# Low parts on VectorE instead of GpSimd, and a layer border without decoding, in a fused retention and two-layer MLP kernel

## The chip, the core and the metric

The kernel runs on one core of a Trainium2 chip. The metric is the device time of one execution in microseconds (us). Three runs of the kernel before gave 601.18, 601.47 and 603.46, a median of 601.47. One more execution was taken with the hardware profiler and is the source of every row below.

The engines are named as in the profile: PE is TensorE (matmuls), PEld its weight loads, DVE is VectorE, ACT is ScalarE, POOL is GpSimd, SP is the engine that issues the transfers here. SBUF is the on-chip memory; PSUM holds what PE writes.

## The reference

A retention (linear attention with a decay for each head), and then two MLP layers over its 1536 tokens of 512 values:

```
for t in range(S):                       # B=2, H=8, S=768, D=64
    state = gamma * state + k[t] (x) v[t]
    y[t] = scale * q[t] @ state
x = y as 1536 x 512
h = x @ w_in;  x = (max(h,0) + alpha*min(h,0)) @ w_out          # layer 1, d_ff = 2048
h = x @ w_in;  P = a0 + a1 h + a2 h^2 + a3 h^3                  # layer 2, d_ff = 2048
Q = 1 + |b0||h| + |b1| h^2;  out = (P / (Q + 1e-6)) @ w_out
```

The eight-byte weights are read as pairs of 32-bit words.

## The kernel before

**Retention.** 12 chunks of 128 tokens, six for each batch element. A chunk has a stage "b" (`att_b`: scores `sc` on PE, DVE multiplies them by the decay mask into `s` at L131, ACT scales q for the state at L136, and POOL multiplies q by `dq_sb` at L137) and a stage "c" (`att_c`: state products `st`, output `y` on PE at L160 and L170, DVE adds `st` to the state `R` at L177 or L179, ACT copies `y` to the high part `xh` at L183, DVE writes the low part `xl` at L184). `att_k` scales k on POOL (L118). Chunks 0 to 4 stand in a prologue; a table `stages` puts the others between the steps of layer 1.

**Splitting.** A matmul operand is a high part (a rounded copy) and a low part (what the copy left over), and each product is three matmuls: high by high, high by low, low by high. So whatever feeds PE (x, the weights, the activations g) is copied by ACT and then subtracted by DVE or POOL.

**Decoding.** 64 weight halves of 128x512 (two layers, 16 ff tiles m, n=0 for w_in and n=1 for w_out) come in as word pairs `r` by SP (L240). Decoding one takes ACT L248 (the absolute value), three DVE operations on the words (L254, L258, L262), ACT L273 (the high part `wh`) and one subtraction at L280 (the low part `wl`). L279 chooses its engine: POOL for every n=1, for the first four ff tiles, and for the halves that start late; else DVE. The table `START` says in which half step a decoding begins; its word operations come one half step later, the copy two, the low part three.

**Steps.** 96 steps, each an ff tile m for a block of 512 tokens: `pe_h` (12 matmuls, L305), the activation, `pe_out` (12 matmuls into four PSUM accumulators, L322). `SWEEPS` orders them: in layer 1 the first `GA` ff tiles (list A) for blocks 0 and 1 with partial sums spilled, then all 16 for block 2, then the rest (list B) for blocks 1 and 0, added to the spilled sums. Layer 2 does likewise with `GC` = 10, blocks 2, 1 and then 0. `pe_h` runs two steps ahead of `pe_out`. In layer 1 the activation is ACT L340 and L341, DVE L346, ACT L351, DVE L356. In layer 2 it is ACT L367 to L369, DVE L373, ACT L380 and L381, DVE L382, L383, L391, L392, L395, ACT L402 (high part of g) and POOL L404 (its low part). `evac` ends a sweep; where it adds (L419) in layer 1 it also makes the two parts of the next layer's x at once, the high part on ACT (L431) and the low one on POOL (L433).

Everything is emitted in one hand-written order (`manual_schedule`), and each engine works through its own queue in that order. Half step 2i stands before `pe_out(i)` and 2i+1 behind it. Tiles share 42 slots of SBUF, and the oldest free one is used next.

Of the kernel before, what the change touches and what calls it, by code (L numbers as in the profile page):

```python
# [7 lines left out]
F32 = mybir.dt.float32  # L8
# [3 lines left out]
ALU = mybir.AluOpType  # L12
# [6 lines left out]
NK = 4  # L19
NCH = 12  # L20
# [3 lines left out]
QC = 1.0 + 1e-6  # L24
NWARM = 8
NSLOT = 42
GA = 6
GC = 10


# [1 line left out]
def tile_fused(  # L32
# [18 lines left out]
    nc = tc.nc  # L51
# [9 lines left out]
    def alloc(nm, dt=F32):  # L61
        k = free.pop(0)
        t = one.tile([P, 1024], dt, tag=f"s{k}", name=nm)
        slot[id(t)] = (k, t)
        return t

    def drop(t):
        free.append(slot.pop(id(t))[0])
# [13 lines left out]
    dq_sb = one.tile([P, 512], F32, tag="dq", name="dq_sb")  # L82
# [5 lines left out]
    def xs(hl, b, ks, sl):  # L88
        return (xh, xl)[hl][b][:, ks, sl]
# [30 lines left out]
    def att_b(c, bank):  # L120
        a = att[c]
        ps = [bank(f"sc{c}_{e}") for e in range(2)]
        for j in range(NK):
            js = slice(j * P, (j + 1) * P)
            for e in range(2):
                es = slice(64 * e, 64 * e + 64)
                nc.tensor.matmul(ps[e][:, js], a["t"][es, js], a["q"][es, js], start=True, stop=True)  # L127
        a["s"] = alloc(f"s{c}")
        for e in range(2):
            es = slice(512 * e, 512 * e + 512)  # L130
            nc.vector.tensor_tensor(out=a["s"][:, es], in0=ps[e], in1=dm_sb[:, es], op=ALU.mult)  # L131
        if c % CPB > 0:
            for j in range(NK):
                js = slice(j * P, (j + 1) * P)
                o = 8 * CPB + 4 * (c % CPB) + j
                nc.scalar.mul(a["q"][:, js], a["q"][:, js], cst_sb[:, o:o + 1])  # L136
            nc.gpsimd.tensor_tensor(out=a["q"], in0=a["q"], in1=dq_sb, op=ALU.mult)  # L137

    def att_c(c, ybank, pbank):
        a = att.pop(c)  # L140
# [51 lines left out]
    Z = {}  # L192
# [5 lines left out]

    A, B = range(0, GA), range(GA, NF)
    C, D = range(0, GC), range(GC, NF)  # L200
# [9 lines left out]
    first, final = {}, {}  # L210
# [5 lines left out]
    START = {}  # L216
    for m in A:
        START[0, m, 0], START[0, m, 1] = 2 * m - 9, 2 * m - 4
    for j, m in enumerate(B):
        START[0, m, 0], START[0, m, 1] = 8 + 4 * j, 10 + 4 * j  # L220
    for m in range(NF):
        for n in range(2):
            k = 2 * m + n
            if k < 8:
                t = 52 + 3 * k
            elif k < 20:
                t = 76 + (5 * (k - 8)) // 3
            else:
                t = 98 + (11 * (k - 20)) // 2
            START[1, m, n] = t  # L230
    SEQ = sorted(START, key=lambda e: (START[e], e))
    loaded = [0, 0]

    def load_next(depth):
        while loaded[0] < len(SEQ) and loaded[0] - loaded[1] < depth:
            k = loaded[0]
            loaded[0] += 1
            l, m, n = SEQ[k]
            r = alloc(f"r{k}", U32)
            nc.sync.dma_start(out=r, in_=SRC[l][n][m].bitcast(U32))  # L240
            words = r.rearrange("p (f t) -> p f t", t=2)
            raw[k] = (words[:, :, 0], words[:, :, 1], r)
# [7 lines left out]
    def w_word(k, part):  # L250
        lo, hi, r = raw[k]
        zu = Z[k].bitcast(U32)
        if part == 0:
            nc.vector.tensor_scalar(  # L254
                out=zu, in0=zu, scalar1=3, scalar2=None, op0=ALU.logical_shift_left
            )
        elif part == 1:
            nc.vector.scalar_tensor_tensor(  # L258
                out=zu, in0=lo, scalar=29, in1=zu, op0=ALU.logical_shift_right, op1=ALU.bitwise_or
            )  # L260
        else:
            nc.vector.scalar_tensor_tensor(  # L262
                out=zu, in0=hi, scalar=0x80000000, in1=zu, op0=ALU.bitwise_and, op1=ALU.bitwise_or
            )
            drop(r)
            loaded[1] += 1
# [9 lines left out]
    def w_lo(k):  # L276
        l, m, n = SEQ[k]
        hi, lo = W[l, m, n]
        eng = nc.gpsimd if n or (l == 0 and m < 4) or START[SEQ[k]] >= 2 * N1 else nc.vector  # L279
        eng.tensor_tensor(out=lo, in0=Z[k], in1=hi.bitcast(F32), op=ALU.subtract)  # L280
        if k % 2 == 1:
            drop(ZP[k // 2])

# [7 lines left out]
    acc = {}  # L291
# [3 lines left out]
    ALL = slice(0, TB)  # L295
# [111 lines left out]
    def evac(i):  # L407
        l, b, m, _, how = STEPS[i]
        if how == "add" or (how == "final" and l == 0):
            part_b = part.pop((l, b), None)  # L410
        else:
            part_b = [alloc(f"p{i}_{n}") for n in range(2)]
        if how == "spill":
            part[l, b] = part_b
        if part_b:
            ps = [part_b[k // 2][:, 512 * (k % 2):512 * (k % 2) + 512] for k in range(NK)]
        for k in range(NK):
            if how == "add":
                nc.vector.tensor_tensor(out=ps[k], in0=acc[0][k], in1=ps[k], op=ALU.add)  # L419
            elif how == "spill" or l == 1:  # L420
                if k % 2 == 0:
                    nc.scalar.copy(ps[k], acc[0][k])
                else:
                    nc.vector.tensor_copy(ps[k], acc[0][k])
            if how != "spill" and l == 1:
                t0 = b * TB + k * P
                nc.sync.dma_start(out=out[t0:t0 + P, :], in_=ps[k])
            if how != "spill" and l == 0:
                src = ps[k] if how == "add" else acc[0][k]
                hap = xs(0, b, k, ALL)  # L430
                nc.scalar.copy(hap, src)  # L431
                eng = nc.gpsimd if how == "add" else nc.vector
                eng.tensor_tensor(out=xs(1, b, k, ALL), in0=src, in1=hap.bitcast(F32), op=ALU.subtract)  # L433
        if how != "spill" and part_b:
            for t in part_b:
                drop(t)


    def rbank(nm):
        return ring.tile([P, 512], F32, tag="ring", name=nm)  # L440
# [4 lines left out]
    N1 = NB * NF  # L445
# [7 lines left out]
    def half(t, scalar_last=None, between=None):  # L453
        evs = dec.get(t, ())

        def each(nm):
            return [e[1] for e in evs if e[0] == nm]

        for e in each("abs"):
            w_abs(e)  # L460
        for e in each("hi"):
            w_hi(e)
        if scalar_last:
            scalar_last()
        for e in each("word"):
            w_word(e, 0)
        for e in each("lo"):
            w_lo(e)
        for e in each("word"):
            w_word(e, 1)  # L470
        if between:
            between()
        for e in each("word"):
            w_word(e, 2)
        load_next(4 if t < 2 * N1 else 2)

    with tc.manual_schedule():
# [3 lines left out]
        ps = rbank("warm")  # L481
# [42 lines left out]


        stages = {-4: ("c", 4)}
        for c in range(5, NCH):
            t = 3 * (c - 5) - 3 + (c > 7)
            stages[t] = ("b", c)
            stages[t + 2] = ("c", c)  # L530

        def stage(t):
            if t not in stages:
# [119 lines left out]
```

## Time and profile before

| what | value |
|---|---|
| median of 3 runs | 601.47 us (601.18 to 603.46) |
| the profiled execution, its span | 605.27 us, 603.5 us |
| PE busy | 581.3 us (96%), 2944 matmuls |
| DVE busy | 484.7 us (80%), 688 operations |
| ACT busy | 360.4 us (60%) |
| POOL busy | 157.9 us (26%), 121 operations |
| mean granted PE clock | 0.988 |

Busy shares are means over stages with different limits, and PE's own are modelled ends of pipelined matmuls; the tables by stretch below count matmuls, which is a better measure of what PE got done. A table by stretch gives the busy us of each engine and the number of its operations, then the granted clock, the share of the DMA engines and GB/s. A chain of waits gives the start, the us on the chain, and what stood there. A timeline gives start, duration, engine, line and operation, then idle time before it and what ended it in brackets.

### The profile page before, as it was taken

To read this page: it belongs to the slowest core of one execution; us is meant where nothing else is said; L and a number is where in the kernel's file an instruction comes from. 1 tells how busy PE (TensorE), PEld (TensorE's weight loads), DVE (VectorE), ACT (ScalarE), POOL (GpSimd) and SP (SyncE) were. 2 spreads that over 40 slices of the span, in tenths; PEclk is the share of its full clock that TensorE was granted. 3 is DMA by queue.
4 is the path that set the end of the run, shared out by engine and by line. 5 is a ranking of instruction groups with operands and counts; after the bars stand their busy time and mean duration, and the time that the engine had idled before them with its cause. 6 is when DMAs were issued, how large, how long until landed. Compare 5 with 4: busy or idle time off the path is not lost.

```text
span 603.5 us, 7942 instructions
## 1 busy us (share of the span) xinstructions
PE 581.3 (96%) x2944; PEld 475.5 (79%) x2944; DVE 484.7 (80%) x688; ACT 360.4 (60%) x637; POOL 157.9 (26%) x121
## 2 busy tenths in 40 slices
PE   7797899999999999999999799999999999999997
PEld 7676778888888888888888578878887888888885
DVE  3979877887777446455887999999999999987786
ACT  3545445555544445445565677777778777776673
POOL 2543331210101000004021443233323332322220
PEclk8999899999999999999999989999999999999999
DMA  8995433223341211211342001011102100010011
GB/s 302 363 401 210 141 104 106 71 70 106 105 141 36 70 36 35 71 49 60 136 140 104 1 36 35 2 36 35 35 1 71 35 1 1 1 70 2 31 40 71
DMA packets 18760, 50.64 MB, mean 84 GB/s; under 512 B 2592, under 2 KB 2592, under 8 KB 18720
## 3 DMA queue, kind: packets, MB, share of 16 engines
q1 hardware_dynamic: 18720, 50.13, 23.8%
q8 instruction: 23, 0.38, 0.2%
q14 instruction: 17, 0.14, 0.1%
HBM read 46.97 MB, written 3.15 MB: 83 GB/s over the span
## 4 chain that ended last, share of the span: by engine, by line
PE 64%; DVE 21%; ACT 7%; issue 5%; DMA 1%; POOL 1%; SPq 0%; DVEq 0%; ACTq 0%; POOLq 0%
PE h L305 30%; PE acc L322 30%; DVE as L392 3%; DVE z L258 3%; DVE as L373 3%; DVE as L391 2%; ACT rr L380 2%; ACT rr L381 2%; DVE z L262 2%; DVE z L254 1%; PE y L160 1%; PE sc L127 1%; PE y L170 1%; DVE as L395 1%; DMA kv<-in_kn_dram 1%
## 5 line engine op out<-in xcount | busy, mean ns | idle before, releaser
L305 PE MATMUL h<-xl,wh 128*128 128x512 f32 x384 | 150.7, 393 | 1.8 <-DVE xl L184 1.8
L305 PE MATMUL h<-xh,wh 128*128 128x512 f32 x384 | 151.6, 395 | 0.0
L305 PE MATMUL h<-xh,wl 128*128 128x512 f32 x384 | 150.5, 392 | 0.0
L322 PE MATMUL acc<-wh,g 128*128 128x512 f32 x384 | 128.1, 395 | 5.4 <-ACT g L402 4.4
L322 PE MATMUL acc<-g,wh 128*128 128x512 f32 x384 | 118.9, 391 | 0.0
L280 POOL TENSOR_TENSOR wl<-z,wh 128x512 fp32r<-128x512 f32 x42 | 60.0, 1430 | 188.9 <-ACT wh L273 178.9
L404 POOL TENSOR_TENSOR g<-as,g 128x512 fp32r<-128x512 f32 x46 | 60.9, 1323 | 155.4 <-ACT g L402 123.9
L322 PEld LDWEIGHTS acc<-wh,g 128*128 128x128 f32 x384 | 71.9, 189 | 24.4 <-ACT g L402 5.3
L305 PEld LDWEIGHTS h<-xl,wh 128*128 128x128 f32 x384 | 72.8, 190 | 17.0 <-DVE xl L184 2.1
L305 PEld LDWEIGHTS h<-xh,wl 128*128 128x128 f32 x384 | 72.8, 190 | 15.4
L305 PEld LDWEIGHTS h<-xh,wh 128*128 128x128 f32 x384 | 72.8, 189 | 15.5 <-issue 0.2
L322 PEld LDWEIGHTS acc<-g,wh 128*128 128x128 f32 x384 | 71.7, 188 | 15.1 <-ACT z L248 0.2
L273 ACT CAST wh<-z 128x512 fp32r<-128x512 f32 x64 | 39.6, 618 | 71.7 <-DVE z L262 71.7
L322 PE MATMUL acc<-wl,g 128*128 128x512 f32 x192 | 75.2, 392 | 0.0
L322 PE MATMUL acc<-g,wl 128*128 128x512 f32 x192 | 74.9, 390 | 0.2 <-POOL wl L280 0.2
L346 DVE SCALAR_TENSOR_TENSOR np<-np,nalpha_sb 128x512 f32<-128x512 f32 x48 | 36.7, 764 | 38.0 <-ACT np L341 38.0
L356 DVE TENSOR_TENSOR g<-np,g 128x512 fp32r<-128x512 f32 x48 | 42.2, 879 | 24.6 <-ACT g L351 22.8
L258 DVE SCALAR_TENSOR_TENSOR z<-r,z 128x512 uint32<-128x512 uint32 x64 | 55.0, 859 | 1.7
L340 ACT ACTIVATE np<-h 128x512 f32<-128x512 f32 x48 | 28.6, 595 | 46.1 <-PE h L305 46.1
L262 DVE SCALAR_TENSOR_TENSOR z<-r,z 128x512 uint32<-128x512 uint32 x64 | 47.6, 744 | 1.7
L373 DVE SCALAR_TENSOR_TENSOR as<-as,bb_sb,rr 128x512 f32<-128x512 f32 x48 | 42.0, 876 | 8.4 <-ACT rr L368 8.4
L392 DVE SCALAR_TENSOR_TENSOR as<-as,ab_sb,rr 128x512 f32<-128x512 f32 x48 | 48.4, 1008 | 0.0
(53 smaller groups left out, 775.0 us busy)
## 6 DMA issues: line engine op xcount, KB each, us to landing
r<-in_w1i_dram SPq DMA_DIRECT2D x16, 512.0 KB, 4.1
r<-in_w1o_dram SPq DMA_DIRECT2D x16, 512.0 KB, 4.2
r<-in_w2i_dram SPq DMA_DIRECT2D x16, 512.0 KB, 3.3
r<-in_w2o_dram SPq DMA_DIRECT2D x16, 512.0 KB, 3.2
qk<-in_qT_dram SPq DMA_DIRECT2D x12, 256.0 KB, 5.6
qk<-in_kT_dram SPq DMA_DIRECT2D x12, 256.0 KB, 6.0
kv<-in_kn_dram SPq DMA_DIRECT2D x12, 256.0 KB, 5.8
kv<-in_vn_dram SPq DMA_DIRECT2D x12, 256.0 KB, 6.2
```

The lines of the kernel that those rows point to most:

```text
L258: nc.vector.scalar_tensor_tensor(out=zu, in0=lo, scalar=29, in1=zu, op0=ALU.logical_shift_right, op1=ALU.bitwise_or)
L262: nc.vector.scalar_tensor_tensor(out=zu, in0=hi, scalar=0x80000000, in1=zu, op0=ALU.bitwise_and, op1=ALU.bitwise_or)
L273: nc.scalar.copy(hi, Z[k])
L280: eng.tensor_tensor(out=lo, in0=Z[k], in1=hi.bitcast(F32), op=ALU.subtract)
L305: nc.tensor.matmul(ps, w[:, ks], xs(hl, b, k, ALL), start=(n == 0), stop=(n == 11))
L322: nc.tensor.matmul(acc[0][k], a, c, start=(begin and n == 0), stop=(end != "" and n == 2))
L340: nc.scalar.activation(n, h, AF.Relu, scale=-1.0)
L346: nc.vector.scalar_tensor_tensor(out=p, in0=n, scalar=nalpha_sb[:, m:m + 1], in1=p, op0=ALU.mult, op1=ALU.add)
L356: nc.vector.tensor_tensor(out=gl, in0=p, in1=gh.bitcast(F32), op=ALU.subtract)
L373: nc.vector.scalar_tensor_tensor(out=s, in0=s, scalar=bb_sb[:, 1:2], in1=r, op0=ALU.mult, op1=ALU.add)
L392: nc.vector.scalar_tensor_tensor(out=a, in0=a, scalar=ab_sb[:, 0:1], in1=r, op0=ALU.add, op1=ALU.mult)
L404: eng.tensor_tensor(out=gl, in0=a, in1=gh.bitcast(F32), op=ALU.subtract)
```

## The change

1. The low parts of the weights and the product of q with `dq_sb` are always made by DVE. POOL keeps L118 and the low part of g in layer 2.
2. Where a layer 1 sweep ends by adding, the two parts of the next x are no longer made there. Their four pieces go on a list, `later`; each even half step takes one, ACT copying and DVE subtracting.
3. `GA` is 5 instead of 6, and list B has eleven ff tiles, whose decodings start every 3.4 half steps instead of every 4, from half step 6.
4. Layer 2's first 20 weight halves start at 52, 56, ... 72 and then at every half step from 76 to 89 (before: to 94); the other 12 start from 100, every 5.25 half steps (before: from 98, every 5.5).
5. The stages of chunks 5 to 11 have a table of their own, up to three half steps earlier.

Lines move by one to ten: L305 becomes L304, L322 L321, L280 L279, L346 L345, L356 L355, L373 L372, L404 L403, L419 L418, and the split of x is at L440 and L441.

```diff
-GA = 6
+GA = 5
...
-            nc.gpsimd.tensor_tensor(out=a["q"], in0=a["q"], in1=dq_sb, op=ALU.mult)
+            nc.vector.tensor_tensor(out=a["q"], in0=a["q"], in1=dq_sb, op=ALU.mult)
...
-        START[0, m, 0], START[0, m, 1] = 8 + 4 * j, 10 + 4 * j
+        START[0, m, 0], START[0, m, 1] = 6 + (17 * j) // 5, 8 + (17 * j) // 5
...
-            elif k < 20:
-                t = 76 + (5 * (k - 8)) // 3
+            elif k < 20:
+                t = 76 + k - 6
             else:
-                t = 98 + (11 * (k - 20)) // 2
+                t = 100 + (21 * (k - 20)) // 4
...
-        eng = nc.gpsimd if n or (l == 0 and m < 4) or START[SEQ[k]] >= 2 * N1 else nc.vector
-        eng.tensor_tensor(out=lo, in0=Z[k], in1=hi.bitcast(F32), op=ALU.subtract)
+        nc.vector.tensor_tensor(out=lo, in0=Z[k], in1=hi.bitcast(F32), op=ALU.subtract)
...
+            if how == "final" and l == 0:
+                split_x(b, k, acc[0][k])
+        if how == "add" and l == 0:
+            for k in range(NK):
+                later.append((b, k, ps[k], part_b[k // 2] if k % 2 else None))
...
+    def split_x(b, k, src, t=None):
+        hap = xs(0, b, k, ALL)
+        nc.scalar.copy(hap, src)
+        nc.vector.tensor_tensor(out=xs(1, b, k, ALL), in0=src, in1=hap.bitcast(F32), op=ALU.subtract)
...
+        if later and t % 2 == 0:
+            split_x(*later.pop(0))
...
-            t = 3 * (c - 5) - 3 + (c > 7)
+        for c, t, u in ((5, -3, -2), (6, -1, 1), (7, 2, 4), (8, 5, 7), (9, 8, 10), (10, 11, 13), (11, 14, 15)):
```

DVE's queue at the start, before: from the low part `xl` of chunk 5 to the scores of chunk 6. `r`, `z`: weight words; `np`, `g`: activation of a step; `s`: masked scores; `wl`: low part of a weight.

```order
L184 TENSOR_TENSOR xl_79<-y_469,xh_76 128x4x128
L254 TENSOR_SCALAR z_431<-z_431 128x512
L258 SCALAR_TENSOR_TENSOR z_431<-r_309,z_431 128x512
L262 SCALAR_TENSOR_TENSOR z_431<-r_309,z_431 128x512
L346 SCALAR_TENSOR_TENSOR np_495<-np_495,nalpha_sb 128x512
L254 TENSOR_SCALAR z_490<-z_490 128x512
L258 SCALAR_TENSOR_TENSOR z_490<-r_379,z_490 128x512
L356 TENSOR_TENSOR g_521<-np_495,g_521 128x512
L262 SCALAR_TENSOR_TENSOR z_490<-r_379,z_490 128x512
L131 TENSOR_TENSOR s_540<-sc_0_530,dm_sb 128x512
L131 TENSOR_TENSOR s_540<-sc_1_531,dm_sb 128x512
```

The same place now, from the `xl` of chunk 5:

```order
L184 TENSOR_TENSOR xl_79<-y_470,xh_76 128x4x128
L131 TENSOR_TENSOR s_501<-sc_0_491,dm_sb 128x512
L131 TENSOR_TENSOR s_501<-sc_1_492,dm_sb 128x512
L254 TENSOR_SCALAR z_431<-z_431 128x512
L279 TENSOR_TENSOR wl_0_275<-z_337,wh_0_274 128x512
L258 SCALAR_TENSOR_TENSOR z_431<-r_309,z_431 128x512
L262 SCALAR_TENSOR_TENSOR z_431<-r_309,z_431 128x512
L345 SCALAR_TENSOR_TENSOR np_509<-np_509,nalpha_sb 128x512
L254 TENSOR_SCALAR z_504<-z_504 128x512
L279 TENSOR_TENSOR wl_3_507<-z_431,wh_3_506 128x512
L258 SCALAR_TENSOR_TENSOR z_504<-r_379,z_504 128x512
```

The scores of chunk 6 follow the low part of chunk 5 at once now. From there to the low part of chunk 6 the queue holds 22 rows before (its last ones are `R` and `xl`) and 15 now: fewer decodings stand in between, and in exchange low parts `wl` do.

PE's queue at chunk 11, before and now: the last output of the retention and what comes next. `acc`: the accumulators of `pe_out`; `h`: those of `pe_h`, which here reads the block that chunk 11 completes.

```order
L160 MATMUL y_1186<-s_1136,kv_990 64x128 x8
L170 MATMUL y_1186<-qk_989,R 128x128 x4
L322 MATMUL acc_0_995<-g_1123,wh_3_492 128x512 x2
L322 MATMUL acc_0_995<-g_1123,wl_3_493 128x512
L322 MATMUL acc_1_996<-g_1123,wh_3_492 128x512 x2
```

```order
L160 MATMUL y_1115<-s_1095,kv_944 64x128 x8
L170 MATMUL y_1115<-qk_943,R 128x128 x4
L304 MATMUL h_1140<-xh_77,wh_0_274 128x512
L304 MATMUL h_1140<-xl_80,wh_0_274 128x512
L304 MATMUL h_1140<-xh_77,wl_0_275 128x512
```

The 12 matmuls of a `pe_out` that followed are gone from this place: the `pe_h` that needs chunk 11's `xh` and `xl` is next.

DVE's queue at the layer border, before: from the adds of the last layer 1 sweep to the end of step 49's activation.

```order
L419 TENSOR_TENSOR p_1_928<-acc_3_2385,p_1_928 128x512
L382 TENSOR_TENSOR as_2785<-as_2785,h_2763 128x512
L383 SCALAR_TENSOR_TENSOR as_2785<-as_2785,ab_sb,h_2763 128x512
L254 TENSOR_SCALAR z_2724<-z_2724 128x512
L280 TENSOR_TENSOR wl_9_2782<-z_2724,wh_9_2781 128x512
L258 SCALAR_TENSOR_TENSOR z_2724<-r_2647,z_2724 128x512
L262 SCALAR_TENSOR_TENSOR z_2724<-r_2647,z_2724 128x512
L391 SCALAR_TENSOR_TENSOR as_2785<-as_2785,rr 128x512
L392 SCALAR_TENSOR_TENSOR as_2785<-as_2785,ab_sb,rr 128x512
L395 SCALAR_TENSOR_TENSOR as_2785<-as_2785 128x512
```

And now:

```order
L418 TENSOR_TENSOR p_1_877<-acc_3_2325,p_1_877 128x512
L381 TENSOR_TENSOR as_2793<-as_2793,h_2776 128x512
L382 SCALAR_TENSOR_TENSOR as_2793<-as_2793,ab_sb,h_2776 128x512
L390 SCALAR_TENSOR_TENSOR as_2793<-as_2793,rr 128x512
L391 SCALAR_TENSOR_TENSOR as_2793<-as_2793,ab_sb,rr 128x512
L394 SCALAR_TENSOR_TENSOR as_2793<-as_2793 128x512
L441 TENSOR_TENSOR xl_78<-p_0_876,xh_75 128x512
```

Four decoding operations no longer stand inside this activation, and the first piece of the deferred split stands behind it.

## Rows read from the trace of the kernel before

**Rows 1.** Table by stretch: length; PE, PEld, DVE, ACT, POOL; clock, DMA share, GB/s.

```profile
36.60:71.60 35.00, 30.07 (x203) 23.65 (x204) 33.64 (x42) 18.68 (x37) 14.74 (x11) 0.95 0.69 250
330.00:360.00 30.00, 25.54 (x107) 20.30 (x106) 29.15 (x39) 20.02 (x35) 14.48 (x11) 0.94 0.05 18
350.00:540.00 190.00, 189.47 (x829) 154.84 (x829) 182.69 (x250) 141.96 (x235) 64.97 (x47) 1.00 0.07 23
540.00:570.00 30.00, 30.00 (x134) 24.86 (x133) 23.50 (x36) 20.03 (x34) 6.51 (x5) 1.00 0.09 32
```

**Rows 2.** Chain of waits: start, us on the chain, what.

```profile
43.63 1.68 DVE z L258
...
59.11 0.34 DVE z L254
59.45 0.60 DVE wl L280
...
62.77 1.31 PE sc L127 x14
...
127.59 2.72 PE h L305 x12
```

**Rows 3.** One line's operations: count, ns min/median/max.

```profile
L258 DVE SCALAR_TENSOR_TENSOR z<-r,z x64: 679/693/1772, 18.9 to 518.9; 128x512 uint32<-128x512 uint32 x64
L392 DVE SCALAR_TENSOR_TENSOR as<-as,ab_sb,rr x48: 737/747/1847, 332.8 to 594.1; 128x512 f32<-128x512 f32 x48
L383 DVE SCALAR_TENSOR_TENSOR as<-as,ab_sb,h x48: 747/748/750, 328.8 to 592.8; 128x512 f32<-128x512 f32 x48
L280 DVE TENSOR_TENSOR wl<-z,wh x22: 681/684/1771, 59.4 to 339.3; 128x512 fp32r<-128x512 f32 x22
```

**Rows 4.** Timeline of DVE and POOL, first and last stretched operations of the start.

```profile
38.59 1.30 POOL L137 TENSOR_TENSOR qk<-qk,dq_sb 128x512 f32<-128x512 f32 x1 [6.76 <-ACT qk L136]
38.93 1.25 DVE L254 TENSOR_SCALAR z<-z 128x512 uint32<-128x512 uint32 x1
...
52.82 1.50 POOL L118 TENSOR_TENSOR kv<-kv,cst_sb 128x512 f32<-128x512 f32 x1
53.33 1.53 DVE L356 TENSOR_TENSOR g<-np,g 128x512 fp32r<-128x512 f32 x1
...
69.95 1.61 DVE L356 TENSOR_TENSOR g<-np,g 128x512 fp32r<-128x512 f32 x1
```

**Rows 5.** Groups by line: count, busy us and mean ns, idle before.

```profile
L280 POOL TENSOR_TENSOR wl<-z,wh 128x512 fp32r<-128x512 f32 x42 | 60.0, 1430 | 188.9 <-ACT wh L273 178.9 <-DMA r<-in_w2i_dram 10.0
L137 POOL TENSOR_TENSOR qk<-qk,dq_sb 128x512 f32<-128x512 f32 x10 | 13.5, 1352 | 54.7 <-ACT qk L136 30.7 <-issue 23.6 <-ACT xh L183 0.5
```

**Rows 6.** Timeline after chunk 8's output: the two parts of x.

```profile
89.06 0.59 ACT L183 CAST xh<-y 128x512 fp32r<-128x512 f32 x1 [2.64 <-PE y L170]
89.94 0.69 DVE L184 TENSOR_TENSOR xl<-y,xh 128x512 fp32r<-128x512 f32 x1
```

**Rows 7.** Timeline in layer 1, step 35's low part and its `pe_out`.

```profile
258.45 0.69 DVE L356 TENSOR_TENSOR g<-np,g 128x512 fp32r<-128x512 f32 x1
266.15 0.61 PE L322 MATMUL acc<-g,wh 128*128 128x512 f32 x2
```

**Rows 8.** Timeline at the border.

```profile
336.54 5.68 POOL L433 TENSOR_TENSOR xl<-p,xh 128x512 fp32r<-128x512 f32 x4
339.31 1.77 DVE L280 TENSOR_TENSOR wl<-z,wh 128x512 fp32r<-128x512 f32 x1
341.01 1.77 DVE L258 SCALAR_TENSOR_TENSOR z<-r,z 128x512 uint32<-128x512 uint32 x1
346.46 0.50 PE L322 MATMUL acc<-wh,g 128*128 128x512 f32 x1 [3.99 <-ACT g L402]
```

**Rows 9.** Timeline in layer 2, stretched operations.

```profile
359.68 1.78 DVE L392 SCALAR_TENSOR_TENSOR as<-as,ab_sb,rr 128x512 f32<-128x512 f32 x1
368.09 1.78 DVE L373 SCALAR_TENSOR_TENSOR as<-as,bb_sb,rr 128x512 f32<-128x512 f32 x1
```

More of the change, by code (lines that the diff above doesn't have):

```diff
@@ L223, in tile_fused @@
             k = 2 * m + n
-            if k < 8:
-                t = 52 + 3 * k
+            if k < 6:
+                t = 52 + 4 * k
             elif k < 20:
-                t = 76 + (5 * (k - 8)) // 3
+                t = 76 + k - 6
             else:
-                t = 98 + (11 * (k - 20)) // 2
+                t = 100 + (21 * (k - 20)) // 4
             START[1, m, n] = t
@@ L427, in evac @@
                 nc.sync.dma_start(out=out[t0:t0 + P, :], in_=ps[k])
[L428 to L434, printed above, removed]
+            if how == "final" and l == 0:
[3 more added lines that the diff above has]
+                later.append((b, k, ps[k], part_b[k // 2] if k % 2 else None))
+        elif how != "spill" and part_b:
             for t in part_b:
                 drop(t)
+    later = []
+    def split_x(b, k, src, t=None):
+        hap = xs(0, b, k, ALL)
+        nc.scalar.copy(hap, src)
+        nc.vector.tensor_tensor(out=xs(1, b, k, ALL), in0=src, in1=hap.bitcast(F32), op=ALU.subtract)
+        if t is not None:
+            drop(t)
     def rbank(nm):
@@ L526, in tile_fused @@
         stages = {-4: ("c", 4)}
-        for c in range(5, NCH):
-            t = 3 * (c - 5) - 3 + (c > 7)
+        for c, t, u in ((5, -3, -2), (6, -1, 1), (7, 2, 4), (8, 5, 7), (9, 8, 10), (10, 11, 13), (11, 14, 15)):
             stages[t] = ("b", c)
-            stages[t + 2] = ("c", c)
+            stages[u] = ("c", c)
         def stage(t):
```

## The prediction

> **What bounds the kernel now.** I read the table by stretch first. In an undisturbed stretch PE issues 134 matmuls in 30 us [rows 1], and twelve of them, a `pe_h` or a `pe_out`, take 2.72 us on the chain [rows 2]; so a matmul is 0.227 us and a step (24) 5.44 us. Against that rate PE falls behind in three places. At the start of layer 1 (36.6 to 71.6) it is busy 30.07 of 35.00 us at a granted clock of 0.95, while DVE is busy for 33.64. At the border (330 to 360) it issues 107 matmuls where 134 would fit: 27 x 0.227 = 6.1 us lost. In layer 2 (350 to 540) it is busy 189.47 of 190, with DVE at 182.69: a balance that DVE just loses [rows 1]. So DVE is the second limit at all three places, and I ask what makes it long.
>
> The chain of waits answers for the start: between 43 and 63 us DVE stands on it, until a PE row (62.77, scores) ends that [rows 2]. Its rows differ: the same L258 takes 1.68 at 43.63, and a low part 0.60 at 59.45. One line's operations give the reason a size: L258 and L392 have a median of 0.69 and 0.75 and a maximum of 1.77 and 1.85, while L383, which reads `h` from PSUM, never leaves 0.747 to 0.750. L280 on DVE is 0.684, with a maximum of 1.77 [rows 3]. The timeline gives the culprit: DVE's L254 at 38.93 and L356 at 53.33 are long, and beside each a POOL operation runs (L137 from 38.59, L118 from 52.82). A long operation is one that shares its time with a POOL operation [rows 4]. Between 36.6 and 71.6 ten DVE operations are long, the first and the last in [rows 4]; by what POOL ran, eight belong to L280 and L137, two to L118.
>
> The Trainium skill, page "SBUF — State Buffer", section "SBUF: two separate sides", says that GpSimd and a VectorE operation with two SBUF inputs share one pair of ports as an exclusive lock, held for a whole instruction, and that the other engine is fully blocked meanwhile. The trace agrees on who is hit (L383 is not); what it shows of the size is about one microsecond per meeting, less than POOL's 1.43 us. By that rule taking work from POOL frees more than it adds.
>
> **The change part by part.**
>
> *Low parts and L137 move to DVE.* POOL loses 42 L280 (60.0 us, 1.43 each), 10 L137 (1.35 each) [rows 5] and the eight low parts of x (the four of the second sweep take 5.68 us, [rows 8]). DVE gets these 60, at 0.68 [rows 3], or 0.60 from one to the next where they queue [rows 2]. That is +36 us of DVE in all, against about 50 us by which I find 56 long operations too long over the kernel, nearly 40 of it by the moved POOL lines. What counts is where.
>
> *Start, first sweep.* Removed: eight meetings of 0.92 each (L356 at 69.95 takes 1.61, undisturbed 0.69) = -7.4. Added up to 71.6: two L137 and four more low parts, 6 x 0.60 = +3.6. Moved: list A's sixth tile leaves this stretch and list B comes in at other places, which makes one decoding less up to the last scores: 0.34 [rows 2] + 2 x 0.69 [rows 3] and the small gaps between, -1.75. The order agrees: 15 rows from chunk 5's low part to chunk 6's, 22 before. Sum -5.5. PE bounds it: what can be won there is its idle 4.9 us plus 5% clock of 35 (1.75) = 6.7. Just outside this stretch I add -0.5 before and -0.4 behind it, where PE also waits for word operations or a low part. Transfers: list B's words are asked for two half steps earlier and 15% denser. DMA has ended 10.0 of 188.9 us of POOL's idle time before a low part, all of it in layer 2 [rows 5], and the share here is 0.69 [rows 1]; I cost it at nothing, with +1 as bound.
>
> *A new wait at chunk 11.* `pe_h` of the block that chunk 11 completes follows its output directly. It needs `xh` and `xl`: after a `y`, 0.59 on ACT and then 0.69 on DVE, with hand-offs 1.6 us in all (89.06 to 90.63) [rows 6]. High-by-high matmuls need only `xh`, but the second one needs `xl`. I take +1.4; bounds 0.6 (`xl` hidden) and 2.5 (DVE late by one or two queued operations). Behind the wait in PE's queue stands all of the next step. **Start in all: -6.4 + 1.4 = -5.0**, bounds -7 and -1.
>
> *Layer 1, middle.* Two sweeps of spare time: step 35's `g` is ready at 259.14 and its `pe_out` starts at 266.15, 7 us later [rows 7]. Low parts (0.60 each, 2 per 6.8 half steps) use none of PE's time here: cost 0. For half steps 76 to 89 the new table starts a decoding in every half step: two per step, each 0.34 + 3 x 0.60 by queue cadence, and the activation 0.66 + 0.60 make 5.5 to 5.7 us of DVE against 5.44. Seven steps of +0.2 eat 1.4 of 7 us, with the early dip perhaps 5: cost 0. By full durations (0.34 + 3 x 0.69 twice, 0.75 + 0.69) it would be 6.3 us, 6 us too much over seven steps, and with the spare time partly used already a stall of up to 4.5: that is a bound, and a rival.
>
> *Border.* Before, step 49's activation has four decoding operations inside it, two of them long (L280 and L258, 1.77 each) since POOL is making low parts of x for 5.68 us at that time; PE waits 3.99 us for `g` [rows 8]. All of it goes: 0.34 + 1.77 + 1.77 + 0.69 is 4.6 us on this one chain, more than the wait. Also, POOL's low part of step 49's `g` is no longer queued behind four others. What is late next is the add of the last accumulators and the activation itself, which needs the new `h` as before. In exchange each of the next four steps gets one copy (0.6 ACT) and one subtraction (0.6 DVE) with no decoding in them; a layer 2 step without decoding takes 23.5 / 30 of DVE [rows 1], so 1.2 us per step is free and hides it; without that cover it would be 4 x 0.6 = +2.4. The deferred pieces belong to a block that is read only two sweeps later, so no PE waits for them. Of 6.1 lost I keep 0.4: **-5.7**, bounds -6.5 and -2.5 (the second stall stays).
>
> *Layer 2.* Twelve decodings remain there, before and now. A step without one needs 23.5 / 30 of DVE [rows 1], 4.26 of 5.44 us: 1.18 is to spare. Before, a decoding costs DVE 1.75 for its words (as above), a meeting of 1.03 of its L280 (L392 at 359.68, 1.78 for 0.747; twelve such), and half a meeting of an L404 (L373 at 368.09; six such) [rows 3, 9]: 3.3 in 2.75 steps, which spare 3.25. Just short, as the stretch shows. Now it costs 1.75 + 0.60 + 0.5 = 2.9 in 2.625 steps, which spare 3.1. Of about 2 us that PE loses there I give back **-0.8**, since a single step can still come late; bounds -2 and, should each new low part meet an L404, 1.03 x 12 less those 0.2 each, +8 (rival 3).
>
> *Nothing else.* `GA` moves a step from one sweep to another; the number of matmuls is the same. L118 stays on POOL, with its two meetings.
>
> Sum: -5.0 - 5.7 - 0.8 = -11.5; I take -11.2, with 0.3 of the +1 for transfers. The profiled execution took 605.27 (span 603.5), so its like now is 594.1. The median of before is 601.47, 3.8 below the profiled one; with the same difference the forecast is **590.3**.
>
> **Rivals.**
>
> 1. *The start is limited by something else.* In the chain, PE and ACT stand right behind DVE, the half clock at 63 to 67 us comes from gaps that may form elsewhere, and 69% DMA share is high [rows 1]. Then the start itself gives nothing, and border and layer 2 still give: 601.5 - 6.5 + 1.4 (the new wait uncovered) = 596.4. Against: DVE is busy 33.64 of 35.
>
> 2. *The dense decoding before the border.* DVE really needs 6.3 us per step in half steps 76 to 92 and PE stalls 4.5 us: 590.3 + 4.5 = 594.8. For it: the full durations. Against: cadence in the chain, 0.60 per operation.
>
> 3. *The meetings move to L404.* POOL keeps its 46 low parts of `g`, and in layer 2 each of the 12 new low parts on DVE meets one. A decoding then needs 2.9 + 1.03 = 3.9 against 3.1 to spare: 12 x 0.8, less the 1.5 us by which `g` can be early, is +8. With the start's -5.0 and the border's -5.7: 598.8. For it: most of the 47 POOL operations of the stretch stay [rows 1]. Against: of the DVE operations that could meet an L404 six did, and a meeting belongs to a POOL operation, of which there are fewer.
>
> 4. *Slower: DVE just gets 60 more operations.* If long operations come from DVE's own two-input work or from DMA traffic rather than from POOL, nothing is freed. Then the start adds 3.6 - 0.4 = +3.2, half steps 76 to 92 +4.5, layer 2 12 x 0.6 = +7.2, and the border gives -4: 601.5 + 11 = 612. It decides once fewer than 4 of the start's ten long operations vanish. Against: L383, and all ten meet a POOL operation.
>
> That the change does not do what it says is excluded by the order: the four border rows are gone.
>
> **Chances.** The forecast has 0.62, with a range of its own of 586.5 to 594.5; rival 1 0.17, rival 2 0.10, rival 3 0.06, rival 4 0.05. Cut at 10% on either side, 586 to 598 holds the first three. A measurement of this kernel tells about 0.5% (3 us) from no change, so faster means under 598.5: the first three less a tail, 0.87; same 0.08 (rival 3 and that tail); slower 0.05.
>
> **What would show it.** DVE operations near 1.7 us only beside L118 and L404, and two instead of ten at the start; the row of scores at 62.77 comes near 55 to 56; a PE gap of about 1.4 us before the `pe_h` behind chunk 11; DVE close to full, but no PE gap, at half steps 76 to 92; about 132 matmuls in the 30 us around the border. Wrong: long DVE operations at the old number without those POOL lines, a PE gap waiting for `wl`, or a gap just ahead of the border.

## The result and the profile after

Four executions of the changed kernel took 593.75 to 595.20 us, median 594.36, against 602.18 for the kernel before beside them: ratio 0.987 (95% interval 0.9843 to 0.9897). With five more on another occasion (592.95; ratio 0.9839, 0.9815 to 0.9864) its nine executions have a median of 593.75, and 57 of the kernel before one of 602.88. So it is 7.8 to 9.5 us faster; 11.2 less, 590.3, was forecast.

The table by stretch of the changed kernel (columns as in [rows 1]):

```profile
36.60:71.60 35.00, 32.20 (x250) 25.86 (x250) 31.75 (x52) 20.30 (x43) 5.62 (x4) 1.00 0.71 258
330.00:360.00 30.00, 30.00 (x134) 24.82 (x134) 29.32 (x46) 24.05 (x41) 8.47 (x6) 1.00 0.06 18
350.00:540.00 190.00, 190.00 (x840) 157.36 (x839) 177.93 (x265) 143.33 (x240) 47.79 (x35) 1.00 0.09 28
```

The border has its full 134 matmuls (107 in [rows 1]), and from 350 to 540 us there are 840 (829 there): no wait of PE is left between 130 and 580 us. DVE does 15 more operations in those 190 us in 4.8 us less. One line's operations (count, ns min/median/max, first and last start, shape):

```profile
L258 DVE SCALAR_TENSOR_TENSOR z<-r,z x64: 679/689/1532, 19.7 to 503.2; 128x512 uint32<-128x512 uint32 x64
L391 DVE SCALAR_TENSOR_TENSOR as<-as,ab_sb,rr x48: 735/746/748, 327.0 to 582.3; 128x512 f32<-128x512 f32 x48
L279 DVE TENSOR_TENSOR wl<-z,wh x64: 678/685/937, 25.4 to 508.8; 128x512 fp32r<-128x512 f32 x64
```

L391 is the L392 of [rows 3], with a maximum of 0.748 in place of 1.847; 64 low parts on DVE have a median of 0.685. Call a DVE operation long when it takes at least 0.35 us more than the shortest of its line. Of 56 long ones 9 are left, six beside L118 and three beside L403, which are the two lines POOL kept; a few more beside L403 are lengthened by less (the 0.937 of L279 is one).

The border in the timeline (start, us, engine, line; the counterpart of [rows 8]):

```profile
335.46 0.69 DVE L394 SCALAR_TENSOR_TENSOR as<-as 128x512 f32<-128x512 f32 x1
336.07 0.69 DVE L441 TENSOR_TENSOR xl<-p,xh 128x512 fp32r<-128x512 f32 x1
336.19 0.63 ACT L401 CAST g<-as 128x512 fp32r<-128x512 f32 x1 [0.47 <-DVE as L394]
336.94 1.63 POOL L403 TENSOR_TENSOR g<-as,g 128x512 fp32r<-128x512 f32 x1 [4.78 <-ACT g L401]
...
339.11 0.39 PE L321 MATMUL acc<-wh,g 128*128 128x512 f32 x1
```

Step 49's high part of `g` is ready at 336.82, 2.29 us before its `pe_out`, and its low part, which the third matmul is the first to read, at 338.57, 0.54 us before it: the chain fits, narrowly. At the start it looks different. The timeline of the changed kernel behind chunk 5's output:

```profile
43.64 0.41 DVE L254 TENSOR_SCALAR z<-z 128x512 uint32<-128x512 uint32 x1
43.98 0.68 DVE L279 TENSOR_TENSOR wl<-z,wh 128x512 fp32r<-128x512 f32 x1
44.28 0.58 ACT L183 CAST xh<-y 128x512 fp32r<-128x512 f32 x1
44.58 0.68 DVE L258 SCALAR_TENSOR_TENSOR z<-r,z 128x512 uint32<-128x512 uint32 x1
45.18 0.68 DVE L355 TENSOR_TENSOR g<-np,g 128x512 fp32r<-128x512 f32 x1
45.79 0.68 DVE L262 SCALAR_TENSOR_TENSOR z<-r,z 128x512 uint32<-128x512 uint32 x1
46.39 0.68 DVE L184 TENSOR_TENSOR xl<-y,xh 128x512 fp32r<-128x512 f32 x1
...
47.12 0.50 PE L304 MATMUL h<-xh,wh 128*128 128x512 f32 x1 [2.17 <-DVE xl L184]
```

`xh` is ready at 44.9, but `xl` stands behind two more queued operations and PE waits 2.17 us. And behind chunk 11 (the counterpart of [rows 6]):

```profile
112.09 0.58 ACT L183 CAST xh<-y 128x512 fp32r<-128x512 f32 x1 [3.05 <-PE y L170]
112.71 0.69 DVE L184 TENSOR_TENSOR xl<-y,xh 128x512 fp32r<-128x512 f32 x1 [2.33 <-ACT xh L183]
112.73 0.50 PE L304 MATMUL h<-xh,wh 128*128 128x512 f32 x1 [0.68 <-ACT xh L183]
113.46 0.50 PE L304 MATMUL h<-xl,wh 128*128 128x512 f32 x1 [0.23 <-DVE xl L184]
```

That is the new wait: 0.91 us of gaps, and with the first matmuls behind them some 1.3 us.

### The profile page after: what moved, and what is told of

Read it like the earlier page. It is cut to its first block, busy times and chain, and to the rows that moved or that the text cites. A ratio compares the mean times of both kernels' runs of the same rounds, so it can differ in the third digit from the quotient of the medians.

```text
span 592.0 us, 7896 instructions
## 1 busy us (share of the span) xinstructions
PE 574.3 (97%) x2944; PEld 473.1 (80%) x2944; DVE 475.8 (80%) x748; ACT 358.9 (61%) x637; POOL 75.8 (13%) x61
## 4 chain that ended last, share of the span: by engine, by line
PE 90%; DVE 4%; DMA 3%; issue 1%; ACT 1%; SPq 0%; DVEq 0%; ACTq 0%
PE h L304 44%; PE acc L321 43%; PE y L170 1%; PE y L160 1%; PE sc L127 1%; DMA kv<-in_kn_dram 1%; DMA qk<-in_kT_dram 1%; DMA dq_sb<-in_dq_dram 1%; DVE xl L184 1%; PE st L149 1%; DVE R L179 1%; DVE p L418 0%; DVE s L131 0%; DVE z L258 0%; DVE as L391 0%
## 5 line engine op out<-in xcount | busy, mean ns | idle before, releaser
L304 PE MATMUL h<-xh,wh 128*128 128x512 f32 x384 | 150.9, 393 | 2.8 <-DVE xl L184 2.2
L304 PE MATMUL h<-xl,wh 128*128 128x512 f32 x384 | 150.4, 392 | 2.8 <-DVE xl L184 2.8
L304 PE MATMUL h<-xh,wl 128*128 128x512 f32 x384 | 150.0, 391 | 0.0
L321 PE MATMUL acc<-wh,g 128*128 128x512 f32 x384 | 125.9, 390 | 0.4 <-ACT g L401 0.4
L403 POOL TENSOR_TENSOR g<-as,g 128x512 fp32r<-128x512 f32 x46 | 62.8, 1364 | 453.6 <-ACT g L401 420.1
L321 PE MATMUL acc<-g,wh 128*128 128x512 f32 x384 | 118.7, 390 | 0.0
L304 PEld LDWEIGHTS h<-xh,wh 128*128 128x128 f32 x384 | 72.4, 188 | 18.6 <-DVE xl L184 2.4
L304 PEld LDWEIGHTS h<-xl,wh 128*128 128x128 f32 x384 | 72.5, 189 | 18.3 <-DVE xl L184 3.4
L321 PEld LDWEIGHTS acc<-wh,g 128*128 128x128 f32 x384 | 72.0, 188 | 16.2 <-ACT g L401 0.9
L304 PEld LDWEIGHTS h<-xh,wl 128*128 128x128 f32 x384 | 72.6, 189 | 15.1
L321 PEld LDWEIGHTS acc<-g,wh 128*128 128x128 f32 x384 | 71.7, 188 | 15.0
L273 ACT CAST wh<-z 128x512 fp32r<-128x512 f32 x64 | 39.6, 619 | 66.5 <-DVE z L262 66.0
L321 PE MATMUL acc<-g,wl 128*128 128x512 f32 x192 | 74.7, 389 | 0.0
L321 PE MATMUL acc<-wl,g 128*128 128x512 f32 x192 | 74.7, 389 | 0.0
L345 DVE SCALAR_TENSOR_TENSOR np<-np,nalpha_sb 128x512 f32<-128x512 f32 x48 | 35.9, 748 | 40.3 <-ACT np L340 39.9
L366 ACT ACTIVATE as<-h 128x512 f32<-128x512 f32 x48 | 28.6, 595 | 39.4 <-PE h L304 39.4
L355 DVE TENSOR_TENSOR g<-np,g 128x512 fp32r<-128x512 f32 x48 | 34.6, 721 | 17.5 <-ACT g L350 17.2
L372 DVE SCALAR_TENSOR_TENSOR as<-as,bb_sb,rr 128x512 f32<-128x512 f32 x48 | 38.0, 792 | 12.4 <-ACT rr L367 12.4
L262 DVE SCALAR_TENSOR_TENSOR z<-r,z 128x512 uint32<-128x512 uint32 x64 | 46.7, 729 | 1.5
L258 DVE SCALAR_TENSOR_TENSOR z<-r,z 128x512 uint32<-128x512 uint32 x64 | 44.9, 702 | 1.0
L279 DVE TENSOR_TENSOR wl<-z,wh 128x512 fp32r<-128x512 f32 x64 | 45.0, 703 | 0.0
```

The source lines that it names most:

```text
L258: nc.vector.scalar_tensor_tensor(out=zu, in0=lo, scalar=29, in1=zu, op0=ALU.logical_shift_right, op1=ALU.bitwise_or)
L262: nc.vector.scalar_tensor_tensor(out=zu, in0=hi, scalar=0x80000000, in1=zu, op0=ALU.bitwise_and, op1=ALU.bitwise_or)
L273: nc.scalar.copy(hi, Z[k])
L279: nc.vector.tensor_tensor(out=lo, in0=Z[k], in1=hi.bitcast(F32), op=ALU.subtract)
L304: nc.tensor.matmul(ps, w[:, ks], xs(hl, b, k, ALL), start=(n == 0), stop=(n == 11))
L321: nc.tensor.matmul(acc[0][k], a, c, start=(begin and n == 0), stop=(end != "" and n == 2))
```

## Experiments

Two quantities sort them. From the start of `pe_h` of step 36 to that of step 52 are 16 steps, undisturbed 16 x 5.44 = 87.04 us; from there to step 84 are 32, 174.08. What goes beyond is the loss at the border and in layer 2; the start of step 36 holds what the start lost.

```
us                          step 36   border loss   layer 2 loss   median of the runs
kernel before               257.99       6.3            2.2         602.88 (57 runs)
  again                     254.77       6.3            2.3         602.16
changed kernel              254.79       0.0            0.0         594.36
  again                     255.23       0.0            0.0         592.95
engine only                 254.98       6.1            0.0         600.91
order only                  259.12       1.5            4.1         601.70
L137 on GpSimd              252.93       0.0            0.0         597.04
split at the border         255.74       8.1            0.1         601.26
decoding at the border      256.28       2.9            1.8         598.75
chunk 11 earlier            251.76       0.0            0.0         590.74
chunk 3 first               253.79       0.0            0.0         593.68
chunks 11 and 5             252.93       0.0            0.0         590.60
chunks 11, 5 and 3          252.17       0.0            0.0         590.49
fewer word operations       250.00       0.0            0.0         587.33
```

Losses at border and layer 2 come out the same to the tenth in two profiles of one kernel; the start moves by 3 us between two profiles of the kernel before. So late differences are read from profiles, and what the start is worth from medians, with the late losses taken off.

**Engine only** (the kernel before, two lines changed):

```diff
-        eng = nc.gpsimd if n or (l == 0 and m < 4) or START[SEQ[k]] >= 2 * N1 else nc.vector
-        eng.tensor_tensor(out=lo, in0=Z[k], in1=hi.bitcast(F32), op=ALU.subtract)
+        nc.vector.tensor_tensor(out=lo, in0=Z[k], in1=hi.bitcast(F32), op=ALU.subtract)
...
-            nc.gpsimd.tensor_tensor(out=a["q"], in0=a["q"], in1=dq_sb, op=ALU.mult)
+            nc.vector.tensor_tensor(out=a["q"], in0=a["q"], in1=dq_sb, op=ALU.mult)
```

> The kernel before, with only its weight low parts and L137 moved from GpSimd to VectorE; group of 6, tables, stages and the split at the border (low part of x on GpSimd) stay. Theory M (most of the gain is meetings of GpSimd and VectorE operations that no longer happen): 8 of the 10 long VectorE operations between 36 and 72 us go, layer 2 has none beside L280; start -3 to -4, border -1 to -2 (four decoding operations still stand in step 49's activation and still meet the low parts of x), layer 2 -2: 595 to 597 us against 602.2. Rival O (most of the gain is where the work stands): the engine alone gives nothing and layer 2 loses up to 7: 602 to 609.

600.91 us, ratio 0.9939 (0.9912 to 0.9966), between the two theories. Layer 2 loses nothing any more, with the old table: the low parts cost nothing on DVE there, as theory M has it. That the engine is all of layer 2 is not shown: behind its border stall of 6.1 us DVE may enter layer 2 with a lead, and the same table and engine behind a shorter stall lose 1.8 (decoding at the border, below). The border keeps its 6.1. Only 7 long operations are left in the whole kernel, four beside L118 and three beside the low parts of x. Yet 600.91 less the late losses (6.1, and 0.6 at the end) is 594.2, and 602.88 less 8.5 is 594.4: the start gained next to nothing. The timeline of DVE and PE, with the kernel before's wait at the same place last, shows one reason:

```profile
54.91 1.53 DVE L279 TENSOR_TENSOR wl<-z,wh 128x512 fp32r<-128x512 f32 x1
56.37 0.68 DVE L258 SCALAR_TENSOR_TENSOR z<-r,z 128x512 uint32<-128x512 uint32 x1
56.97 0.68 DVE L355 TENSOR_TENSOR g<-np,g 128x512 fp32r<-128x512 f32 x1
57.57 0.68 DVE L262 SCALAR_TENSOR_TENSOR z<-r,z 128x512 uint32<-128x512 uint32 x1
58.17 0.85 DVE L177 COPY R<-st 64x256 f32<-64x256 f32 x2
...
59.17 2.04 PE L127 MATMUL sc<-qk 64*128 64x128 f32 x14 [3.37 <-DVE R L177]
...
62.77 1.31 PE L127 MATMUL sc<-qk 64*128 64x128 f32 x14 [1.60 <-DVE R L177]
```

DVE goes through its queue without a gap, a low part stands in it that meets L118, and the wait for `R` is 3.37 us where it was 1.6. Behind it the granted clock is at its lower level, 1.2 GHz (table by stretch, the third number from the end is the clock):

```profile
60.00:64.00 4.00, 4.00 (x17) 3.20 (x16) 3.14 (x6) 3.63 (x8) 0.00 (x0) 0.50 0.83 296
```

**Order only** (the changed kernel with the same two lines put back).

> The changed kernel, with the weight low parts and L137 back on the engines they had before; everything else as changed. Theory M: the meetings come back, some 50 long VectorE operations; start about as before (order -1.75, new wait at chunk 11 +1.3), border -4 to -5, layer 2 as before: 597 to 599. Rival O: as the changed kernel, 594 to 595.

601.70, ratio 0.9972 (0.995 to 0.9995): slower than theory M said, and far from rival O. The border loses 1.5. No operation of step 49's activation is long here; the meetings lie ahead of the border, one long L258 per step in the dense decoding:

```profile
315.98 1.79 DVE L258 SCALAR_TENSOR_TENSOR z<-r,z 128x512 uint32<-128x512 uint32 x1
...
322.28 1.78 DVE L258 SCALAR_TENSOR_TENSOR z<-r,z 128x512 uint32<-128x512 uint32 x1
```

From one to the next DVE needs 6.30 us for a step that takes PE 5.44, and the time by which `g` is early falls from 4.9 us at step 41 to nothing at step 46. That is the stall of the prediction's rival 2; with the low parts on DVE a step there takes 5.67 us, and it does not come. Layer 2 loses 4.1, more than before. The new table stands a little denser there and each decoding meets L280 again, but the shorter stall may also leave DVE a smaller lead; no run separates the two. The two halves give 2 us and 1 us alone, and 8 to 9 together.

**L137 on GpSimd** (in the changed kernel, its line alone put back).

> The changed kernel with only L137 back on GpSimd. Theory M: ten operations of 0.60 to 0.68 leave VectorE and up to ten meetings of 0.9 come back, at the start only: +0 to +2, 594.5 to 596.5, with long VectorE operations beside L137 in the trace. Rival (L137 on VectorE costs more than it frees, since it delays the first low part of x): -0.5 to -1.5, near 593.

597.04, ratio 0.9888 (0.9863 to 0.9912): by the ratios 1 to 3 us slower than the changed kernel. That is 0.5 us above theory M's range, which the scatter of the start covers; the rival falls. Six of its 13 long operations are beside L137, but its one profile is of its fastest execution (591.8, mean clock 0.996; the other seven ran at 0.988 to 0.994), so where the loss lies is not shown.

**The kernel before, again.**

> The kernel before, unchanged, for a second profile of it. The difference of the two profiled executions (605.27 to 593.75) is larger than that of the medians. If the first profile was a costly execution of the kernel before, this one takes 602 to 603, and the missing 2 to 4 us lie in fewer stretches at half clock (four in the first profile) or a shorter stall at the border; start, border and layer 2 lose 12.5, 6 and 2 there, and less here. If the profiler itself costs the kernel before more than it costs the changed one, it is 605 again.

602.16, the profiled execution 602.22. Border and layer 2 lose what they lost in the first profile; step 36 starts at 254.77 instead of 257.99, and three stretches run at the lower clock where the first profile had four. The first profile was a costly execution at the start, 2.4 us above the median of 57, and the working took the start's idle time from it. Chunk 11's low part and the first matmul of step 12's `pe_h` in this profile, and then that matmul in the changed kernel:

```profile
122.40 0.68 DVE L184 TENSOR_TENSOR xl<-y,xh 128x512 fp32r<-128x512 f32 x1
...
124.21 0.39 PE L305 MATMUL h<-xh,wh 128*128 128x512 f32 x1
...
124.23 0.39 PE L304 MATMUL h<-xh,wh 128*128 128x512 f32 x1
```

**Split at the border** (the changed kernel, low part on DVE, but at once):

```diff
-        if how == "add" and l == 0:
-            for k in range(NK):
-                later.append((b, k, ps[k], part_b[k // 2] if k % 2 else None))
-        elif how != "spill" and part_b:
+            if how == "add" and l == 0:
+                split_x(b, k, ps[k])
+        if how != "spill" and part_b:
```

> The changed kernel with the split of the next x made at the end of the sweep again, low part on VectorE. It puts four subtractions (4 x 0.60) and four copies on ACT ahead of step 49's activation, whose low part of g was 0.54 us early and that of step 48 1.51. If the border's gain needs the deferral: PE waits 1 to 2 us at step 49, 595.5 to 596.5 against 594.4, the start and layer 2 as in the changed kernel. Rival (what freed the border is the missing decoding alone): no wait, 594 to 594.5.

601.26, ratio 0.9978 (0.9954 to 1.0001): nearly the whole gain is gone, not 1 to 2 us. PE's longest waits between 270 and 550 us (line and what it waited for: us in total, times, longest), and the clock behind the longest of them:

```profile
PE acc L321 <- ACT g L401: 1.7, 1, 1.7
PE acc L321 <- DVE p L418: 1.2, 2, 1.0
PE acc L321 <- ACT g L350: 0.8, 1, 0.8
PE acc L321 <- POOL g L403: 0.6, 1, 0.6
```

```profile
345.00:350.00 5.00, 3.85 (x9) 2.78 (x10) 4.86 (x8) 4.47 (x8) 1.55 (x2) 0.68 0.01 3
```

The expectation set only DVE's 2.4 us against the spare time. But in this edit each subtraction stands right behind its add, and DVE waits 0.69 us for ACT's copy in between. Here are the first add, the first and the last subtraction, and then the four adds of the changed kernel, merged:

```profile
333.10 0.68 DVE L418 TENSOR_TENSOR p<-acc,p 128x512 f32<-128x512 f32 x1
334.48 1.02 DVE L440 TENSOR_TENSOR xl<-p,xh 128x512 fp32r<-128x512 f32 x1 [0.69 <-ACT xh L439]
...
340.75 0.69 DVE L440 TENSOR_TENSOR xl<-p,xh 128x512 fp32r<-128x512 f32 x1 [0.69 <-ACT xh L439]
...
330.31 2.48 DVE L418 TENSOR_TENSOR p<-acc,p 128x512 f32<-128x512 f32 x4
```

So adds and split take 8.3 us of DVE's queue, where the adds alone took 2.5, and the adds, which free the accumulators, come late too. Of the loss 1.8 us arises at the earlier sweep's end; behind the border the clock falls to a mean of 0.68 for 5 us. Waits of 4.5 us became a loss of 8. A split at once but behind all four adds was not run, so the 8 us are the price of this form.

**Decoding at the border** (the changed kernel with the old table of layer 2).

> The changed kernel with the old table of layer 2's decoding, which puts one into step 49's activation (0.34 + 3 x 0.60 = 2.1 us on VectorE, no meeting with GpSimd now); 0.54 us of that is spare. If place and engine add up: PE waits 1.5 to 2 us at the border, layer 2 loses at most 0.5: 596 to 597. Rival (place alone makes the stall): the old 6.3 us come back, 600. Rival (meetings alone): 594.5.

598.75, ratio 0.9934 (0.9905 to 0.9964), above the expected range: 2.9 at the border, and 1.8 behind it (steps 53 to 61), where at most 0.5 was expected. PE's waits in the same stretch, and what stands around the first:

```profile
PE acc L321 <- ACT g L401: 1.6, 1, 1.6
PE acc L321 <- POOL g L403: 1.4, 3, 0.6
```

```profile
338.95 0.62 ACT L273 CAST wh<-z 128x512 fp32r<-128x512 f32 x1 [4.64 <-DVE z L262]
...
341.72 0.62 ACT L401 CAST g<-as 128x512 fp32r<-128x512 f32 x1
342.39 0.50 PE L321 MATMUL acc<-wh,g 128*128 128x512 f32 x1 [1.63 <-ACT g L401]
```

Both rivals fall. The wait for ACT's `g` is 1.6, within the expected 1.5 to 2, but by luck: the sum of 2.1 less 0.54 used the spare time of the low part, and PE waits here for the high part, which had 2.29 us to spare. It comes 4.0 us later than in the changed kernel (both counted from step 36): 2.3 by the four operations, 1.0 since DVE comes late to this activation, and 0.8 on ACT, whose queue stood 4.64 us at the decoding's copy L273 and then had four operations ahead of L401. It is not 4.0 of waiting as before: there meetings made the same four operations 2.5 us longer.

**Chunk 11 earlier** (the stage entry `(11, 14, 15)` becomes `(11, 12, 14)`).

> The changed kernel with chunk 11 at half steps 12 and 14 instead of 14 and 15, so that a pe_out of 2.72 us stands between its output and the pe_h that reads it. If the wait there is that of the two parts of x: its 0.9 us and the half microsecond lost behind it go, -1.0 to -1.4, 593.0 to 593.4, all of it between 100 and 120 us. Rival: the scores and outputs of chunks 10 and 11 now queue on VectorE one behind the other and the wait comes back elsewhere: 594.4.

590.74, ratio 0.9796 (0.9766 to 0.9825), less than the expected 593.0 to 593.4. The wait is gone, a `pe_out` stands in between:

```profile
107.76 0.59 ACT L183 CAST xh<-y 128x512 fp32r<-128x512 f32 x1 [0.19 <-PE y L170]
...
108.38 0.69 DVE L184 TENSOR_TENSOR xl<-y,xh 128x512 fp32r<-128x512 f32 x1
...
110.32 0.39 PE L304 MATMUL h<-xh,wh 128*128 128x512 f32 x1
```

It beats both kernels. The median falls by 2 to 3.6 us, more than the wait's 1.4; the rest is of the size of the start's scatter, and its cause is not shown.

**Chunk 3 first** (in the prologue, the decoding of the last two half steps behind chunk 3).

```diff
-            half(n - NPRE)
+            if n < 6:
+                half(n - NPRE)
+        half(6 - NPRE)
+        half(7 - NPRE)
         att_k(4)
```

> The changed kernel with the decoding work of one half step put behind chunk 3 instead of ahead of it, so that on VectorE the low part of chunk 3 comes before three word operations and one low part. If the first pe_h waits for that low part because of these: its wait of 2.57 us falls under 0.7 and the stretch up to 36 us loses 1 to 2 us less (more where the half clock behind the wait goes too): 592 to 593.5. Rival: the decoding is what is short there, the next pe_h waits as much longer: 594.4 or more.

593.68: no measurable difference. The wait before the first `pe_h` falls from 2.57 to 0.6, but it is 1.10 in the changed kernel's second profile too, so part of that is scatter; and the scores of chunk 5 then wait 1.45 where it was 0.62.

**Chunks 11 and 5**, and **all three** (the output of chunk 5 ahead of its half step's decoding):

```diff
+            if i == -1:
+                stage(2 * i)
             if 0 <= old < N1:
...
-            stage(2 * i)
+            if i != -1:
+                stage(2 * i)
```

> The changed kernel with chunk 11 at half steps 12 and 14, as before, and the output of chunk 5 taken ahead of the decoding of its half step instead of behind it, so that its low part stands five rows earlier on VectorE. In all kernels with the changed table PE waits 2.2 to 2.4 us for that low part near 44 us. If VectorE's queue is what holds it: that wait falls by 1 to 2 us, 589 to 590. Rival: the five rows (decoding and the first g) are then late instead and a later wait takes it back: 590.7 as with chunk 11 alone.

> The same with chunk 3 ahead of one half step's decoding too. If the three are independent: another -0.7, 588 to 589.5. Rival (the decoding put back there comes late at chunk 5 instead): no better than without, 590.

590.60 (0.9800, 0.9771 to 0.9829) and 590.49 (0.9795, 0.9769 to 0.982): the rivals hold, nothing beyond chunk 11. In the first, the wait of 2.2 us near 44 falls to 0.5, and the next `pe_out` waits for the low part that was put back:

```profile
44.86 0.50 PE L304 MATMUL h<-xh,wh 128*128 128x512 f32 x1 [0.31 <-DVE xl L184]
...
49.73 0.50 PE L321 MATMUL acc<-g,wl 128*128 128x512 f32 x1 [0.95 <-DVE wl L279]
```

**The changed kernel, again.**

> The changed kernel, unchanged, for its median over more executions and a second profile. Border and layer 2 together are 8.5 us shorter than before in the profiles, to the tenth; the start varies by 3 us between executions. If the start gave nothing on the mean: 594 to 595 against 602.5 to 603. If it gave the forecast 5 us: 589 to 590.

592.95, 9.5 below the 602.49 beside it. With both occasions, 602.88 - 593.75 = 9.1, of which 8.5 are border and layer 2: the start gave about 0.6 (-0.7 and 1.0 on the two occasions).

**Fewer word operations** (one early return in `w_word` for the first 14 decodings).

> The changed kernel without L258 in its first 14 decodings (their weights are then other numbers), 14 operations of 0.60 to 0.69 less on VectorE up to 95 us, and every transfer as it was. If VectorE's queue sets the start: the waits before the first pe_h (2.6) and near 44 us (2.2) fall, -2 to -4: 590.5 to 592.5. Rival (transfers set it, the DMA engines being full until about 52 us): 594.4.

587.33, ratio 0.9752 (0.9725 to 0.9778): 5.6 us less than the changed kernel beside it, more than expected. The stretch at the start:

```profile
36.60:71.60 35.00, 34.69 (x253) 27.65 (x253) 28.17 (x49) 20.68 (x42) 6.87 (x5) 1.00 0.73 267
```

PE is busy 34.69 of 35 with every transfer in place: in this stretch DVE's queue sets PE's pace, and the transfers do not. The wait near 44 us falls to 0.31; the one before the first `pe_h` (1.85) lies between those of the changed kernel's two profiles. The 14 operations are 8.4 to 9.7 us of DVE, and 5.6 of them came out at PE.

## Why the prediction was right, and where not

- **What bounds the kernel: right.** DVE is the limit at the start (the experiment with fewer word operations), at the border and in layer 2. Long operations are meetings with POOL: take POOL's lines away and the long operations go with them, 56 to 9 and 7. The reading that two-input operations are hit leaves one out: L254 reads one SBUF tile and is lengthened too (1.25 at 38.93 in [rows 4]; its median is 0.42).
- **Border, forecast -5.7: -6.3.** The whole loss went. The stall was a wait of 3.99 and one of 0.47 us, and a stretch at the lower clock behind it. Each part of the change is needed: the engine (1.5 without it, by the dense decoding ahead of the border), the free chain (2.9 without it) and the deferral (8.1 without it, in the form that was run). The working priced the split at 2.4 us if nothing covers it; undone, it cost the most.
- **Layer 2, forecast -0.8: -2.2.** Need is under spare and nothing is lost; the working kept a remainder that did not come. But the balance alone does not decide: the old table with the low parts on DVE also has need under spare (2.9 against 3.25), and lost 1.8 next to the border, where the deferred pieces stand as well. Meetings with L404 did not multiply, so rival 3 falls: of the six long L373 beside it two are left; why fewer is not shown.
- **Start, forecast -5.0: about -0.6. This is the step that failed.** The new wait at chunk 11 was right: 1.3 for +1.4. The term of -6.4 was not. It counted each meeting removed from DVE's queue as time on PE's path, and took the idle time to be won from one execution that was 2.4 us above the median. Long operations between 36.6 and 71.6 did fall from ten to three, but DVE did 52 operations there instead of 42, and PE gained only 2.1 us of busy time and 0.05 of clock; the wait behind chunk 5's `xl` stayed (2.17, before 1.91), because the operations ahead of it, low parts among them, still fill DVE. The scores at 62.77 came forward to 57.24, nearly as forecast, and chunk 11's low part from 122.40 in the second profile before to 112.71; yet the `pe_h` of step 12 starts at 124.23, and at 124.21 there. So the retention moved ahead and the MLP steps fell back by as much. Where one wait is mended the next takes over, as chunk 5 and chunk 3 showed.
- **From the profile to the median.** Profile to profile the kernel went from 605.27 to 593.75, 11.5 for 11.2. The working carried the 3.8 between profile and median over to the changed kernel; there the difference was 0. That 11.5 came out as summed is luck: from the second profile of the kernel before it is 8.5 (602.22 to 593.75). A good sum in the profile hid a start term that was a matter of that execution.
- **Rivals.** The time 594.4 lies nearest rival 2 (594.8), then rival 1 (596.4), then the forecast (590.3); the sum alone would not tell them apart. Rival 1's premise, that the start gives nothing on balance, held; its cause, a limit other than DVE, did not. Rival 2 fell: step by step the spare time in the dense decoding ahead of the border (steps 38 to 47) stayed at 3.4 us and above. Rival 4 fell with the engine-only kernel: its 52 moved operations (the low parts of x stay on POOL there) left 7 long ones, and layer 2 lost nothing.

## What to carry to other kernels

An operation taken out of a full queue is worth its time only if what stands next on the path moves up with it; ask for each wait which row would end it afterwards. Two edits on one chain do not add: the engine alone gave 2 us, the order alone 1, and both 8 to 9. When spare time is set against a delay, take that of the operand which PE waits for first. Before a term is sized from a stretch that varies, look at a second profile of the same kernel, and forecast the median from the median.

## What the runs showed of the hardware

A wait of PE can cost more than its length: at the border 4.5 us of gaps became a loss of 6.3, with a granted clock of 0.59 behind them in the kernel before:

```profile
347.82 1.22 PE L322 MATMUL acc<-wh,g 128*128 128x512 f32 x2 [0.47 <-POOL g L404]
...
347.00:351.00 4.00, 3.53 (x10) 2.57 (x10) 3.78 (x5) 2.96 (x7) 2.01 (x2) 0.59 0.02 4
```

The 0.41 of those 4 us are 1.6 us, by estimate. In order only one gap of 0.97 us, with the clock at 1.00 behind it, cost 1.27.

In layer 2 of the kernel before a meeting costs L392 and L373, operations of 0.75 us, some 1.03 to 1.10 more, beside POOL operations of 1.29 to 1.84 us: never the POOL operation's whole length. The two lines on POOL, over the whole kernel (ns min/median/max):

```profile
L280 POOL TENSOR_TENSOR wl<-z,wh x42: 1264/1301/1838, 23.1 to 524.6; 128x512 fp32r<-128x512 f32 x42
L404 POOL TENSOR_TENSOR g<-as,g x46: 1279/1301/1618, 335.3 to 587.5; 128x512 fp32r<-128x512 f32 x46
```
